# Attention into two feed-forward stages: the opening's order of work, first key loads and zero fills

## The chip, the core and the metric

The kernel runs on one core of a Trainium2 chip. The metric is the device time of one execution in microseconds (us), as the median of the runs shown. The engines are TensorE (PE, matrix products and transposes through it), VectorE (DVE), ScalarE (ACT), GpSimd (POOL) and SyncE (SP, which issues most transfers). Each works through its own instructions in order, and they wait for one another by semaphores.

## The reference

Two batches, eight heads, 768 tokens, head size 64. Queries meet the keys of a window and, beside them, one key per block of 32 (the blocks' maxima); values likewise (the blocks' means). The result, 1536 tokens by 512, goes through two dense stages.

```python
def _attn_ref(q, k, v):
    k_sum = k.reshape(B, H, nb, block, D).max(axis=3)
    v_sum = v.reshape(B, H, nb, block, D).mean(axis=3)
    scores_l = scale * np.matmul(q, k.transpose(0, 1, 3, 2))
    mask_l = np.abs(pos[:, None] - pos[None, :]) < window
    scores_s = scale * np.einsum('bhsd,bhnd->bhsn', q, k_sum)
    scores_s = scores_s + np.log(block)
    scores_l_m = np.where(mask_l, scores_l, -1000000000.0)
    scores_all = np.concatenate([scores_l_m, scores_s], axis=-1)
    scores_all = scores_all - np.max(scores_all, axis=-1, keepdims=True)
    a = np.exp(scores_all)
    a = a / (np.sum(a, axis=-1, keepdims=True) + 1e-09)
    return np.matmul(a, np.concatenate([v, v_sum], axis=2))

x = attention as 1536 x 512
x = (x @ w_a) * (x @ w_b) @ w_out      # 512 -> 1536 -> 512
h = x @ w_in                           # 512 -> 2048
out = np.maximum(0.01 * h, h) @ w_out2
```

## The kernel before

**Products.** Every fp32 product of the dense stages is three products of split operands (`mm3`, L741): each operand is a high part and the rest. A weight is brought by SP into one of three staging buffers (`stage`, L364, tile `wst`), then split by a chain of seven steps that are queued in `bg` and taken out a few at a time: L388 on VectorE and L394 on ScalarE read the staged tile, then L400, L403 and L409 on VectorE (the last, the "join", is the last reader of the staging buffer), L416 on ScalarE makes the high part, and L419 on VectorE the rest. The weights come in the order a0, b0, a1, b1, a2, b2, a3, b3, so that the seventh, a3, takes the staging buffer of the fourth, b1.

**Attention.** The work goes by pairs i of 256-token groups. For the first chunk of 512 tokens, pair i is the pair of heads 2i and 2i+1 of batch 0, for two groups j = 0, 1. `load_k` and `load_q` bring keys and queries, `k_prep` transposes keys on TensorE (six transposes, L612, in two PSUM banks), copies them to `kts` on ScalarE (L618, L620), takes the blocks' maxima on VectorE (L623) and copies these beside the keys on GpSimd (L630). `q_prep` transposes queries (L649, L653). `scores` multiplies (L670), takes mask and row minimum on VectorE (L684, one per window) and the exponential on ScalarE (L690). `normal` divides (L699 to L701), `p_transpose` turns the weights (L711, L715), and `pv` multiplies by the windows of values in `vw` (L725) and splits the result into the high part (ScalarE, L735) and the rest (VectorE, L736) of x. The blocks' sums of values are made from `vb` (L553, L567, L589, L596) and put into `vw` by GpSimd (L224). `early(kt)` multiplies the kt-th x of chunk 0 by a0, b0, a1 and b1 (PSUM banks ps_a, ps_b and two ps_c).

**Order.** `attention_ops` gives every operation a number, PER (8) per pair plus an offset (pv is at PV, 13), and the operations are written out in the order of these numbers. A scheduler then sets each engine's order. `tc.issue_after(x)` holds the instructions under it behind x. Transposes and scores take turns on four PSUM banks, in the order in which they are written, so a later one waits for the readers of the fourth before it. The value tiles `vw`, whose unused rows must be zero, are filled by GpSimd before it makes identity and masks (L275).

Of the kernel before, what the change touches and what calls it, by code (L numbers as in the profile page):

```python
# [21 lines left out]
def kernel(  # L22
# [14 lines left out]
    P = 128  # L37
# [100 lines left out]
    def load_k(b, hp):  # L138
        if b > 0 and hp >= NP - 2:
            t = vb_whole[2 * (hp - NP) + 5].rearrange("p j d -> p (j d)")[:, 0 : NTB * 2 * D]  # L140
            t = t.rearrange("p (n c d) -> p n c d", n=NTB, c=2)
        else:
            t = q_p.tile([P, NTB, 2, D], F32, tag="k", name="k", bufs=2)
        for c in range(2):
            with behind_values(b > 0):
                nc.sync.dma_start(
                    out=t[:, :, c, :], in_=k[b, 2 * hp + c].rearrange("(n p) d -> p n d", p=P)
                )
        k_t[b, hp] = t
# [86 lines left out]
    def attention_ops():  # L236
# [3 lines left out]
        for i, p in enumerate(sum(pairs, [])):  # L240
# [5 lines left out]
            for m, (b, hp) in enumerate(dict.fromkeys(x[:2] for x in p)):  # L246
                vi, r = divmod(2 * hp, HV)
                if (b, hp) not in seen:
                    seen.add((b, hp))
                    add(-22 if b > 0 and hp >= NP - 2 else -18, LOAD, load_k, b, hp)  # L250
                    for j in range(2):
                        add(2 * m + j / 4 - 10.5 if (b, hp) == (0, NP - 1) else 2 * m + j - 12, PRODUCT, k_prep, b, hp, j)
# [21 lines left out]
    for t in vw_t:  # L274
        nc.gpsimd.memset(t, 0.0)  # L275
# [94 lines left out]
    def convert():  # L370
# [15 lines left out]
        def low():  # L386
# [6 lines left out]
            with tc.issue_after(pace["turned"].ins):  # L393
                nc.scalar.activation(  # L394
                    out=t["c"].bitcast(F32), in_=hi_w.bitcast(F32), func=AF.Abs, scale=2.0**-112
                )
# [207 lines left out]
    def k_prep(b, hp, j):  # L604
# [5 lines left out]
        with tc.issue_after(st["out"].ins) if (b, hp) == (0, NP - 1) else nullcontext():  # L610
# [12 lines left out]
        nc.vector.tensor_reduce(  # L623
            out=ks_t[hp][:, g * GT // BLK : (g + n) * GT // BLK],
            in_=ps[:, : n * GT].rearrange("p (n j) -> p n j", j=BLK),
            op=ALU.max,
            axis=AX.X,
        )
# [67 lines left out]
    def normal(i, j):  # L696
        pm, sm = st["pm", i, j]
        with behind(i == 0):
            nc.vector.tensor_scalar_add(sm, sm, 1.0e-9)  # L699
# [18 lines left out]
    def pv(i, p):  # L718
# [12 lines left out]
        for j, b, hp, g, n in runs(p):  # L731
# [3 lines left out]
            nc.scalar.copy(out=x[:, 0], in_=src)  # L735
            nc.vector.tensor_tensor(  # L736
                out=x[:, 1], in0=src, in1=x[:, 0].bitcast(F32), op=ALU.subtract
            )

# [54 lines left out]
    ops.append((2.5, LOAD, lambda: [stage() for _ in range(3)], 0))  # L794
    firsts = ((("a", 0), "a"), (("b", 0), "b"), (("a", 1), "c0"), (("b", 1), "c1"))
    for i, x in enumerate(firsts):
        ops.append((PV, LOAD, lambda x=x: first_weights(*x), 0))
    ops.sort(key=lambda o: o[:2])
    rest = []
    for o in ops:  # L800
        if o[0] <= end or o[3] < n_first:
            o[2]()
            if o[1] == PRODUCT and o[0] >= PER+0.5 and (bg or cnt["conv"] < N_FIRST):
# [495 lines left out]
```

## Time and profile before

| what | us |
|---|---|
| runs shown: lowest, median, highest | 636.07, 637.85, 638.39 |
| the profiled execution's own time | 635.28 |
| span of its trace | 633.4 |
| TensorE busy in the span | 611.6 (97%) |
| VectorE busy | 485.4 (77%) |
| ScalarE busy | 317.9 (50%) |
| GpSimd busy | 55.7 (9%) |

The page is of one execution. Its span runs from the first to the last instruction; 1.9 us of its own time lie around it. Busy shares are means over the whole span, and the stretches differ: a view by stretch says which engine is full where. A row of a timeline has the start, the length, the engine, the line, the operation with output and input, and in brackets how long the engine had been idle and for what it is thought to have waited. Where a row has several instructions, its length is from the first's start to the last's end.

### The profile page before, as it was taken

What the parts mean: (1) busy time and instruction counts of PE and PEld (TensorE: products, weight loads), DVE (VectorE), ACT (ScalarE), POOL (GpSimd) and SP (SyncE); (2) the same over time, 40 slices, a digit from 0 to 9 for tenths busy, and PEclk for the clock granted to TensorE, in tenths of its full rate; (3) what the DMA queues carried; (4) which work ended last, traced back from release to release, by engine and by line L of the source; (5) the groups of instructions that cost most, each with busy time, mean ns of one, the idle gap of its engine ahead of it and who ended that gap; (6) DMA issues with size and microseconds to landing.
All of it is one profiled execution on the core that took longest, in us unless ns stands there. A gap on an engine that the chain in (4) does not pass through costs nothing.

```text
span 633.4 us, 9456 instructions
## 1 busy us (share of the span) xinstructions
PE 611.6 (97%) x3344; PEld 498.5 (79%) x3344; DVE 485.4 (77%) x1070; ACT 317.9 (50%) x707; POOL 55.7 (9%) x101
## 2 busy tenths in 40 slices
PE   6589999999999999999999999999999999999997
PEld 4467777777888888888888888877888888888886
DVE  4996987853996869986889999687588576885552
ACT  5677885752545425434453648475463434443320
POOL 5224010000000001202120102000000000000000
PEclk9899999999999999999999999999999999999999
DMA  8989757620124503736593327323133013030013
GB/s 200 257 208 199 160 116 177 191 72 24 45 71 145 136 15 94 139 120 146 142 222 102 89 80 166 95 64 109 35 99 100 14 54 99 1 99 1 0 68 132
DMA packets 81006, 67.85 MB, mean 107 GB/s; under 512 B 47360, under 2 KB 67840, under 8 KB 80960
## 3 DMA queue, kind: packets, MB, share of 16 engines
q1 hardware_dynamic: 75808, 57.95, 31.7%
q0 software_dynamic: 5152, 9.31, 8.8%
q8 instruction: 26, 0.43, 0.3%
q14 instruction: 20, 0.16, 0.1%
HBM read 52.82 MB, written 10.49 MB: 100 GB/s over the span
## 4 chain that ended last, share of the span: by engine, by line
PE 80%; DVE 5%; DMA 5%; ACT 4%; issue 3%; SPq 1%; POOL 1%; POOLq 0%; DVEq 0%; ACTq 0%
PE ps_t L743 34%; PE ps_c L743 17%; PE ps_a L743 12%; PE ps_b L743 11%; PE ps_t L670 2%; DMA wst<-in_moe_w_out_dram 2%; PE ps_t L725 1%; PE ps_t L711 1%; ACT pm L690 1%; DMA neg<-wc 1%; DMA wst<-in_moe_w_a_dram 1%; DVE wc L403 1%; DMA q<-in_q_dram 1%; DVE wc L409 1%; SPq L209 1%
## 5 line engine op out<-in xcount | busy, mean ns | idle before, releaser
L743 PE MATMUL ps_c<-wsp,hs 128*128 128x512 f32 x288 | 75.1, 390 | 1.4 <-ACT acc L860 1.0
L743 PE MATMUL ps_t<-wsp,hs 128*128 128x512 f32 x288 | 74.5, 389 | 0.0
L743 PE MATMUL ps_t<-ys,wsp 128*128 128x512 f32 x270 | 68.2, 389 | 0.0
L394 ACT ACTIVATE wc<-wst 128x512 f32<-128x512 f32 x68 | 45.3, 673 | 45.2 <-DVE wsp L419 17.8
L743 PEld LDWEIGHTS ps_c<-wsp,hs 128*128 128x128 f32 x288 | 53.9, 188 | 13.3 <-ACT acc L860 1.4
L871 DVE TENSOR_TENSOR hs<-h,hs 128x512 fp32r<-128x512 f32 x72 | 49.3, 687 | 18.6 <-ACT hs L870 18.3
L743 PEld LDWEIGHTS ps_t<-wsp,hs 128*128 128x128 f32 x288 | 54.1, 188 | 11.2
L743 PEld LDWEIGHTS ps_t<-ys,wsp 128*128 128x128 f32 x270 | 50.7, 188 | 10.5
L870 ACT CAST hs<-h 128x512 fp32r<-128x512 f32 x72 | 44.5, 621 | 26.0 <-DVE h L1134 18.4
L416 ACT CAST wsp<-wc 128x512 fp32r<-128x512 f32 x68 | 41.8, 620 | 30.6 <-DVE wc L409 30.6
L743 PE MATMUL ps_a<-x,wsp 128*128 128x512 f32 x186 | 51.2, 403 | 4.5 <-ACT x L735 4.1
L743 PE MATMUL ps_t<-x,wsp 128*128 128x512 f32 x222 | 53.2, 389 | 0.0
L743 PE MATMUL ps_b<-x,wsp 128*128 128x512 f32 x192 | 51.7, 398 | 0.0
L1086 DVE TENSOR_TENSOR h<-ps_t,h 128x512 f32<-128x512 f32 x56 | 37.6, 687 | 17.0 <-PE ps_t L743 16.7
L1022 ACT ACTIVATE h<-h 128x512 f32<-128x512 f32 x32 | 20.2, 632 | 57.5 <-DVE h L1086 57.4
L743 PEld LDWEIGHTS ps_t<-x,wsp 128*128 128x128 f32 x222 | 41.7, 188 | 8.6
L403 DVE SCALAR_TENSOR_TENSOR wc<-wc,wr 128x512 int32<-128x512 int32 x68 | 46.5, 686 | 0.7
L409 DVE SCALAR_TENSOR_TENSOR wc<-wst,wc 128x512 int32<-128x512 int32 x68 | 46.6, 686 | 0.6
L743 PEld LDWEIGHTS ps_a<-x,wsp 128*128 128x128 f32 x186 | 33.9, 188 | 13.4 <-ACT x L735 4.6
L419 DVE TENSOR_TENSOR wsp<-wc,wsp 128x512 fp32r<-128x512 f32 x56 | 38.7, 697 | 5.8 <-ACT wsp L416 5.8
L743 PE MATMUL ps_t<-hs,wsp 128*128 128x512 f32 x144 | 42.7, 389 | 0.0
L690 ACT ACTIVATE pm<-pm,nb 128x128 f32<-128x128 f32 x96 | 37.5, 393 | 10.1 <-DVE nb L684 10.0
(129 smaller groups left out, 1098.1 us busy)
## 6 DMA issues: line engine op xcount, KB each, us to landing
wst<-in_moe_w_out_dram SPq DMA_DIRECT2D x28, 512.0 KB, 3.4
wst<-in_moe_w_in_dram SPq DMA_DIRECT2D x16, 512.0 KB, 3.8
wst<-in_moe_w_a_dram SPq DMA_DIRECT2D x12, 512.0 KB, 4.8
wst<-in_moe_w_b_dram SPq DMA_DIRECT2D x12, 512.0 KB, 4.0
y<-acc POOLq DMA_DIRECT2D x16, 256.0 KB, 6.1
y<-acc SPq DMA_DIRECT2D x12, 256.0 KB, 2.3
neg<-wc POOLq DMA_DIRECT2D x12, 256.0 KB, 3.5
acc<-y SPq DMA_DIRECT2D x12, 256.0 KB, 3.1
```

The source lines that it names most:

```text
L394: nc.scalar.activation(out=t["c"].bitcast(F32), in_=hi_w.bitcast(F32), func=AF.Abs, scale=2.0**-112)
L403: nc.vector.scalar_tensor_tensor(out=t["c"], in0=t["c"], scalar=3, in1=t["r"], op0=ALU.logical_shift_left, op1=ALU.bitwise_or,)
L409: nc.vector.scalar_tensor_tensor(out=t["c"], in0=hi_w, scalar=SIGN, in1=t["c"], op0=ALU.bitwise_and, op1=ALU.bitwise_or,)
L416: t["high"] = nc.scalar.copy(out=t["w"][:, 0], in_=t["c"].bitcast(F32))
L419: nc.vector.tensor_tensor(out=t["w"][:, 1], in0=t["c"].bitcast(F32), in1=t["w"][:, 0].bitcast(F32), op=ALU.subtract,)
L670: nc.tensor.matmul(out=ps[h, w, :], lhsT=qt[h, w * W : (w + 1) * W], rhs=kts[h, (g * G + w) * SC : (g * G + w) * SC + P], start=True, stop ...
L690: nc.scalar.activation(out=pm[:, w, :], in_=pm[:, w, :], func=AF.Exp, scale=-1.0, bias=nb[:, w : w + 1], accum_out=sm[:, w : w + 1],)
L743: nc.tensor.matmul(out=ps, lhsT=w(a), rhs=x(b), start=first and j == 0, stop=last and j == 2)
L870: pace["split"] = nc.scalar.copy(out=t[:, 0], in_=src)
L871: nc.vector.tensor_tensor(out=t[:, 1], in0=src, in1=t[:, 0].bitcast(F32), op=ALU.subtract)
L1022: nc.scalar.activation(out=h, in_=src, func=AF.Prelu, alpha=0.01)
L1086: nc.vector.tensor_tensor(out=out, in0=ps, in1=u, op=ALU.add)
```

## The change

Four things are changed, in the order of the diff below.

- **First keys.** The keys of heads 0 and 1 come in four transfers and not two: blocks 0 to 3 and blocks 4 and 5 apart, head 0 issued by SP as before, head 1 by ScalarE ahead of its table load.
- **Third pair's keys.** The load of heads 4 and 5 stands behind the first two staged weights and not ahead of them. Their transposes, and those of heads 6 and 7, are held behind the first pair's pv, and the maxima of heads 4 and 5 behind the rest of the first x (L736).
- **Zeros.** VectorE fills `vw`, ahead of its other fills.
- **First x.** Only a0's conversion is begun ahead of the first pv. ScalarE's first step (L394) of every later weight is held behind the high part of the first x (L735), the second group's normalization of pair 1 behind its rest (L736), and a1 is staged by a step of its own.

The numbers of instructions stay: two fills go from GpSimd to VectorE, and two transfers more are issued.

```diff
@@ load_k
-            with behind_values(b > 0):
-                nc.sync.dma_start(
-                    out=t[:, :, c, :], in_=k[b, 2 * hp + c].rearrange("(n p) d -> p n d", p=P)
-                )
+            src = k[b, 2 * hp + c].rearrange("(n p) d -> p n d", p=P)
+            parts = ((0, 2 * GT // P), (2 * GT // P, NTB)) if (b, hp) == (0, 0) else ((0, NTB),)
+            put = nc.scalar if (b, hp, c) == (0, 0, 1) else nc.sync
+            for n0, n1 in parts:
+                with behind_values(b > 0):
+                    put.dma_start(out=t[:, n0:n1, c, :], in_=src[:, n0:n1])
@@ attention_ops
-                    add(-22 if b > 0 and hp >= NP - 2 else -18, LOAD, load_k, b, hp)
+                    add(-22 if b > 0 and hp >= NP - 2 else -13.4 if (b, hp) == (0, 2) else -18, LOAD, load_k, b, hp)
-                        add(2 * m + j / 4 - 10.5 if (b, hp) == (0, NP - 1) else 2 * m + j - 12, PRODUCT, k_prep, b, hp, j)
+                        at = {(0, 2): j / 4 - 2.5, (0, 3): j / 4 - 10}.get((b, hp), 2 * m + j - 12)
+                        add(at, PRODUCT, k_prep, b, hp, j)
@@
-        nc.gpsimd.memset(t, 0.0)
+        nc.vector.memset(t, 0.0)
@@ low, in convert
-            with tc.issue_after(pace["turned"].ins):
+            with tc.issue_after(pace["turned"].ins if i < 1 else pace["first x"].ins):
@@ k_prep
-        with tc.issue_after(st["out"].ins) if (b, hp) == (0, NP - 1) else nullcontext():
+        with tc.issue_after(st["out"].ins) if b == 0 and hp >= 2 else nullcontext():
...
+        with tc.issue_after(st["low x"].ins) if (b, hp) == (0, 2) else nullcontext():
             nc.vector.tensor_reduce(
@@ normal
-        with behind(i == 0):
+        after = st["low x"].ins if (i, j) == (1, 1) else line[-1]
+        with tc.issue_after(after) if i == 0 or (i, j) == (1, 1) else nullcontext():
@@ pv
+            if i == 0:
+                pace["first x"], st["low x"] = hi, lo
@@
-    ops.append((2.5, LOAD, lambda: [stage() for _ in range(3)], 0))
+    ops.append((2.5, LOAD, lambda: [stage() for _ in range(2)], 0))
+    ops.append((2.7, LOAD, stage, 0))
...
-        ops.append((PV, LOAD, lambda x=x: first_weights(*x), 0))
+        ops.append((PV if i < 1 else PV + 0.5, LOAD, lambda x=x: first_weights(*x), 0))
...
-            if o[1] == PRODUCT and o[0] >= PER+0.5 and (bg or cnt["conv"] < N_FIRST):
+            n_now = 1 if o[0] < PV else N_FIRST
+            if o[1] == PRODUCT and o[0] >= PER+0.5 and (bg or cnt["conv"] < n_now):
```

The scheduler makes new orders of these. TensorE's start of the program, before (line numbers of the kernel before; the four PSUM banks are ps_t, with a number for each use, and kts_91 holds heads 0 and 1):

```order
L612 MATMUL ps_t_187<-ident,k 128x128 x4
L612 MATMUL ps_t_195<-ident,k 128x128 x2
L649 MATMUL ps_t_208<-ident,q 128x128 x4
L612 MATMUL ps_t_217<-ident,k 128x128 x4
L612 MATMUL ps_t_225<-ident,k 128x128 x2
L670 MATMUL ps_t_235<-kts_91,qt 64x128 x8
L649 MATMUL ps_t_264<-ident,q 128x128 x4
L670 MATMUL ps_t_277<-kts_91,qt 64x128 x8
L612 MATMUL ps_t_297<-ident,k 128x128 x4
```

and with the change (line numbers are three to six higher there):

```order
L615 MATMUL ps_t_189<-ident,k 128x128 x4
L615 MATMUL ps_t_197<-ident,k 128x128 x2
L653 MATMUL ps_t_210<-ident,q 128x128 x4
L674 MATMUL ps_t_234<-kts_91,qt 64x128 x8
L615 MATMUL ps_t_219<-ident,k 128x128 x4
L615 MATMUL ps_t_227<-ident,k 128x128 x2
L653 MATMUL ps_t_263<-ident,q 128x128 x4
L674 MATMUL ps_t_279<-kts_91,qt 64x128 x8
L674 MATMUL ps_t_349<-kts_92,qt 64x128 x8
```

The six transposes of the second keys (ps_t 217 and 225 before, 219 and 227 now) stood ahead of the first scores and stand behind them; the third keys' transposes have left this place.

VectorE around the join of the fourth weight, b1, before (L409 is the join; in the lists of VectorE the minima of the scores of pair 2 are left out):

```order
L699 TENSOR_SCALAR sm<-sm 128x4
...
L553 TENSOR_TENSOR vb_103<-vb_103 96x512
L409 SCALAR_TENSOR_TENSOR wc<-wst,wc 128x512
L700 RECIPROCAL sm<-sm 128x4
L400 TENSOR_SCALAR wc<-wc 128x512
L567 TENSOR_REDUCE v_567<-vb_103 96x32 x2
L736 TENSOR_TENSOR x_1_654<-ps_t_637,x_1_654 128x512
```

and with the change, where the join is L412:

```order
L556 TENSOR_TENSOR vb_103<-vb_103 96x512
L704 TENSOR_SCALAR sm<-sm 128x4
L406 SCALAR_TENSOR_TENSOR wc<-wc,wr 128x512
L403 TENSOR_SCALAR wc<-wc 128x512
L570 TENSOR_REDUCE v_569<-vb_103 96x32 x2
L705 RECIPROCAL sm<-sm 128x4
...
L412 SCALAR_TENSOR_TENSOR wc<-wst,wc 128x512
L406 SCALAR_TENSOR_TENSOR wc<-wc,wr 128x512
```

The join now has the sums of values (L570), one reciprocal (L705) and the fifth weight's L403 ahead of it, which stood behind it.

ScalarE from the second value sums on to the third x (x_2), before; the second L394 here is the seventh weight's, a3:

```order
L596 ACTIVATE vs<-ps_t_661 24x256
L653 ACTIVATE qt<-ps_t_710 128x512
L394 ACTIVATE wc<-wst 128x512
L416 CAST wsp<-wc 128x512
L715 COPY pt<-ps_t_671 128x512
L690 ACTIVATE pm,sm<-pm,nb 128x128 x3
L715 COPY pt<-ps_t_732 128x512
L690 ACTIVATE pm,sm<-pm,nb 128x128
L394 ACTIVATE wc<-wst 128x512
L690 ACTIVATE pm,sm<-pm,nb 128x128 x4
L735 CAST x_2_776<-ps_t_759 128x512
```

and with the change, where L397 is that step, the first of the two the sixth weight's:

```order
L419 CAST wsp<-wc 128x512
L397 ACTIVATE wc<-wst 128x512
L720 COPY pt<-ps_t_673 128x512
L397 ACTIVATE wc<-wst 128x512
L657 ACTIVATE qt<-ps_t_712 128x512
L694 ACTIVATE pm,sm<-pm,nb 128x128 x4
L720 COPY pt<-ps_t_734 128x512
L694 ACTIVATE pm,sm<-pm,nb 128x128 x4
L720 COPY pt<-ps_t_790 128x512
L740 CAST x_2_778<-ps_t_761 128x512
```

The seventh weight's first step stood behind the first group's exponentials (L690) of pair 3, and now stands ahead of them and of the fifth queries' copy.

## Rows read from the trace of the kernel before

**Rows 1.** Busy time by stretch of the span; columns are on its first line.

```profile
core 0: us, PE busy (x) PEld busy (x) DVE busy (x) ACT busy (x) POOL busy (x), PEclk, DMA share, GB/s
15.00:30.00 15.00, 8.30 (x90) 6.05 (x88) 14.93 (x45) 10.64 (x34) 3.04 (x3) 0.92 0.90 243
45.00:60.00 15.00, 14.02 (x159) 10.97 (x159) 10.58 (x49) 11.96 (x48) 8.14 (x10) 1.00 0.94 218
120.00:400.00 280.00, 280.00 (x1355) 230.35 (x1354) 226.26 (x434) 136.76 (x261) 24.98 (x28) 1.00 0.42 110
```

**Rows 2.** Timeline of VectorE to 34 us: start, length, instruction, in brackets idle before.

```profile
8.79 1.02 DVE L623 TENSOR_REDUCE ks<-ps_t 128x16 f32<-128x512 f32 x2 [1.45 <-ACT kts L620]
10.56 0.29 DVE L684 CUSTOM_DVE_ANT_0 pm<-ps_t,negm_first 128x128 f32<-128x128 f32 x1 [0.75 <-PE ps_t L670]
...
12.08 0.29 DVE L684 CUSTOM_DVE_ANT_0 pm<-ps_t,negm_mid 128x128 f32<-128x128 f32 x1 [0.58 <-PE ps_t L670]
...
33.03 0.43 DVE L388 TENSOR_SCALAR wr<-wst 128x512 int32<-128x512 uint32 x1 [1.07 <-DMA wst<-in_moe_w_b_dram]
33.80 0.43 DVE L400 TENSOR_SCALAR wc<-wc 128x512 f32<-128x512 f32 x1 [0.34 <-ACT wc L394]
```

**Rows 3.** Timeline of TensorE, first keys and scores.

```profile
4.51 1.51 PE L612 MATMUL ps_t<-ident,k 128*128 128x128 f32 x6 [4.51 <-POOL negm_mid L288]
...
8.43 1.97 PE L670 MATMUL ps_t<-kts,qt 64*64 64x128 f32 x16
...
10.94 1.09 PE L670 MATMUL ps_t<-kts,qt 64*64 64x128 f32 x16
```

**Rows 4.** Timeline of SyncE's queue, the first key transfers.

```profile
0.74 1.02 SPq L146 DMA_DIRECT2D k<-in_k_dram  x2
```

**Rows 5.** Transfers into k issued before 2 us, issue to landing.

```profile
DMA to landing us min/median/max: 2.4/2.8/3.1
```

**Rows 6.** Timeline of GpSimd, the zeros and the first copied key sums.

```profile
0.74 1.84 POOL L275 MEMSET vw<- 128x1024 f32 x2 [0.29 <-POOLq L1281]
...
7.62 0.42 POOL L630 COPY kts<-ks 128x288 f32<-128x288 f32 x1
```

**Rows 7.** Timeline of ScalarE, copies of the second keys and first exponentials.

```profile
8.11 0.48 ACT L618 COPY kts<-ps_t 128x384 f32<-128x384 f32 x1 [0.60 <-PE ps_t L612]
8.49 0.27 ACT L620 COPY kts<-ps_t 128x128 f32<-128x128 f32 x1
...
10.89 0.40 ACT L690 ACTIVATE pm<-pm,nb 128x128 f32<-128x128 f32 x1 [1.80 <-DVE nb L684]
...
12.06 0.57 ACT L653 ACTIVATE qt<-ps_t 128x512 f32<-128x512 f32 x1
```

**Rows 8.** Timeline of VectorE, what stands behind the fourth weight's join.

```profile
39.18 0.68 DVE L409 SCALAR_TENSOR_TENSOR wc<-wst,wc 128x512 int32<-128x512 int32 x1
...
39.87 0.39 DVE L400 TENSOR_SCALAR wc<-wc 128x512 f32<-128x512 f32 x1
40.19 1.10 DVE L567 TENSOR_REDUCE v<-vb 96x32 f32<-96x256 f32 x2
```

**Rows 9.** Transfers into wst issued from 14 to 60 us, issue to landing.

```profile
DMA to landing us min/median/max: 4.9/5.9/6.8
```

**Rows 10.** Timeline of ScalarE, seventh weight, exponentials and third x.

```profile
48.00 0.68 ACT L394 ACTIVATE wc<-wst 128x512 f32<-128x512 f32 x1 [0.38 <-DVE nb L684]
48.58 0.39 ACT L690 ACTIVATE pm<-pm,nb 128x128 f32<-128x128 f32 x1
...
50.12 0.56 ACT L735 CAST x<-ps_t 128x512 fp32r<-128x512 f32 x1
50.63 0.60 ACT L653 ACTIVATE qt<-ps_t 128x512 f32<-128x512 f32 x1
```

**Rows 11.** Timeline of TensorE, the first product of the first x.

```profile
27.67 0.80 PE L743 MATMUL ps_a<-x,wsp 128*128 128x512 f32 x1 [3.64 <-ACT x L735]
```

**Rows 12.** Busy time and granted clock from 27.6 to 30.8 us.

```profile
27.60:30.80 3.20, 3.13 (x17) 2.52 (x19) 3.20 (x7) 1.99 (x7) 0.00 (x0) 0.50 1.12 279
```

More of the change, by code (lines that the diff above doesn't have):

```diff
@@ L622, in k_prep @@
         )
[L623 to L628, printed above, removed]
+        with tc.issue_after(st["low x"].ins) if (b, hp) == (0, 2) else nullcontext():
+            nc.vector.tensor_reduce(
+                out=ks_t[hp][:, g * GT // BLK : (g + n) * GT // BLK],
+                in_=ps[:, : n * GT].rearrange("p (n j) -> p n j", j=BLK),
+                op=ALU.max,
+                axis=AX.X,
+            )
         if g + n == NGB:
@@ L734, in pv @@
             x = x_tile(c, hp)[:, :, t0 : t0 + n * GT]
-            nc.scalar.copy(out=x[:, 0], in_=src)
-            nc.vector.tensor_tensor(
+            hi = nc.scalar.copy(out=x[:, 0], in_=src)
+            lo = nc.vector.tensor_tensor(
                 out=x[:, 1], in0=src, in1=x[:, 0].bitcast(F32), op=ALU.subtract
             )
+            if i == 0:
+                pace["first x"], st["low x"] = hi, lo
     def mm3(ps, w, x, first, last):
```

## The prediction

> **What bounds the kernel now.** I read the busy time by stretch first. From 120 to 400 us TensorE is busy for all 280 us, and from 45 to 60 for 14.02 of 15; from 15 to 30 it is busy for 8.30 only, while VectorE is for 14.93 of 15 [rows 1]. So the end is set by TensorE's work, and time can be won or lost only ahead of some 50 us. There VectorE sets the pace: its timeline shows no gap from 12.08, the minima of the second scores, until it waits 1.07 and 0.34 for the fourth weight at 33 us [rows 2]. What this dense run loses or gains goes through x into TensorE's products, and from there one for one to the end. All four edits lie in this part.
>
> **Start.** The first keys land 2.4 and 3.1 after their issues; SP issues both in 1.02, so at 0.74 and about 1.25, and they land at 3.1 and 4.35 [rows 4, 5]. TensorE's first transposes begin at 4.51, put down to GpSimd, but the second landing is as late [rows 3]. With two queues both issues can stand at 0.74. The gain lies between nothing (the engines that carry the bytes are as full as before) and 4.35 - 3.1 = 1.25; I take 0.8, since the other head's blocks 0 to 3 are all that the first four transposes need. The trace shows with this pair what sharing does: the second landing took 0.7 longer than the first from its issue. The Trainium skill (DMA: Bandwidth & Descriptors, Issuing engines are not separate DMA queues) says that transfers from several engines run on the same 16 DMA engines and that a second issuer saves only the time of issuing; by it the gain would be one issue's half of 1.02, 0.5, and the sum 0.3 higher.
>
> GpSimd would hold this gain up: its first copy of key sums starts at 7.62, right behind its masks, and these began behind 1.84 of zeros [rows 6]. Without the zeros they end by 5.8, and the keys decide. The zeros on VectorE have no row. Between the first instruction at 0.7 and the first maxima, which cannot come before TensorE's transposes at 3.7, VectorE has 3 us for them; as on GpSimd they would take 1.84, and if they were half that, nothing changes. Cost nothing, while they stay below 2. So the first scores come at 7.6 for 8.43 [rows 3], the first minima at 9.75 for 10.56, and the first exponential at 10.1 for 10.89 [rows 2, 7].
>
> **Second keys.** Here the change loses it. Their transposes used TensorE's time ahead of the first scores, and their maxima stood at 8.79 [rows 2]. Now they stand behind these scores, which take 1.97 [rows 3], and ScalarE has three exponentials ahead of their copies: 10.89 to 12.06 before, 1.17 [rows 7]. So the first copies start at 10.1 + 1.17 = 11.25, take 0.65 (8.11 to 8.76) [rows 7], and the first of the two maxima (half of 1.02 and some) ends at 12.5. The second scores wait for that, as they use its PSUM bank. From their start at 10.94 to their minima at 12.08 it was 1.14 [rows 2, 3], so now 13.6. **The dense run begins 1.5 later.** It could be none, if copies or transposes came sooner, and 2.3 if the keys don't land earlier.
>
> **Third pair's keys and first x.** Transposes, copies and maxima are the same in number, later, and inside the dense run: no cost on VectorE. VectorE has fewer steps ahead of the first x's rest, so x comes earlier; TensorE waited 3.64 for it [rows 11]. But b0's rest comes later, and TensorE's next products need that, so I count nothing for the early x by itself. What is won is the wait for the fourth weight: SP issues it with one value load fewer ahead of it, and VectorE meets it later; 1.07 + 0.34 = **1.4 won** [rows 2].
>
> **The seventh weight.** Its staging buffer comes free with the join of the fourth, b1, which ended at 39.18 + 0.60, 27.7 behind 12.08 [rows 2, 8]. The join now has another L400 (0.39) and the value sums (1.10) ahead, which were behind it [rows 8]: less the overlap, 1.4. So it ends at 13.6 + 27.7 - 1.4 + 1.4 = 41.3. Transfers into wst take 4.9 to 6.8, median 5.9 [rows 9]; the weight lands at 46.2 to 48.1, I take 47.2. Before, ScalarE began its L394 at 48.00, behind the first group's exponentials [rows 10]. Now it waits for it ahead of them, and everything behind it on ScalarE waits too: L394 0.58, the queries' copy 0.5, four exponentials 1.54 (48.58 to 50.12), a copy 0.5, four exponentials 1.54, a copy 0.5, then the third x [rows 10]. 47.2 + 5.2 = 52.4, for 50.12: **2.3 later.** VectorE, ready for these exponentials from about 46 on, idles about 2 us, having done more of the conversions.
>
> **Sum.** From the third x on TensorE has 1 us spare in 15 [rows 1], so at most 1 of this is taken up; I take none. The 1.5 and the 1.4 are in the 2.3 already. 635.28 + 2.3 = 637.6 on the profiled execution. The median of the runs shown stands 2.57 above that one: 637.85 + 2.3 = **640.2**.
>
> **Rivals.** *A: faster, no wait at the seventh weight.* If the second keys' copies slip in so that the dense run begins at 12.1 as before, the join ends at 39.8, the transfer can land by 44.7 (4.9), ahead of the exponentials, and what stays is 1.4 won and 1.4 of work brought forward: -2.8, or 635.0; should TensorE also fill a part of its 3.64, 634.3. It decides at the second minima: 12.1 or 13.6. For it speaks that the keys may gain 1.25; against it, that three exponentials stand in the way in the written order. *B: no change.* VectorE's work is the same, and 1.5 lost against 1.4 won is nothing; the weight lands at 46.2 and TensorE's 1 us of spare takes what is left: 637.9. *C: slower by twice as much.* The first scores took 1.97, the later ones 1.09, for the same work [rows 3], and after the wait of 3.64 the granted clock stood at 0.50 (1.2 GHz) from 27.6 to 30.8 [rows 11, 12]. TensorE's opening now has the second keys' transposes (1.51) standing later and two gaps. If the low clock lasts over the second scores too, these and the transposes cost 0.9 + 0.7 more; with keys that gain nothing (0.8) and a seventh weight at the late end (0.8) the sum is 2.3 + 3.2 = 5.5: 643.4. The Trainium skill (TensorE: Matmul & The Clock Gate, Part 1) says that the array starts at half rate and gets the full rate only after sustained work; that this trace shows at its start by the 1.97. *D: the change doesn't do what it says:* the keys land no earlier, all else as forecast: 641.0, inside the range.
>
> **Chances.** Forecast 0.47 (639 to 642), A 0.18, B 0.15, C 0.20. A measurement of this kernel can tell 0.5%, 3.2 us, from no change: below 634.7 is faster, above 641.0 slower. Faster: most of A, 0.14. Slower: C, and the upper third of the forecast with D, 0.37. The same: 0.49. The range, 634.8 to 643.8, holds A's upper part, B, the forecast, and C up to its price.
>
> **What would show it.** Right: first transposes at about 3.7, the second minima at 13.6, b1's join at 41.3, ScalarE idle ahead of L397 until 47.2, the third x's high part at 52.4, and VectorE idle there. Wrong: second minima by 12.1, or a seventh L397 that waits for no transfer, or the products after 60 us standing where they did although the third x is late; then TensorE had room that I did not see. The start's part is wrong if the first transposes still begin at 4.5, the zeros' if VectorE's first maxima wait for its fills.

## The result: 1.2% slower, and the profile after

| what | before | with the change |
|---|---|---|
| median of the runs, us | 637.03 (636.07 to 638.39) | 644.82 (643.84 to 645.21) |
| ratio, 95% interval | | 1.0118 (1.0093 to 1.0144) |
| profiled execution, us | 635.28 | 643.84 |
| span of its trace, us | 633.4 | 642.1 |
| TensorE / VectorE / ScalarE busy, us | 611.6 / 485.4 / 317.9 | 619.3 / 486.6 / 317.8 |

The forecast of 640.2 was 2.3 above 637.85, the median that stands ahead of it. The direction was the forecast's, the size was not: 7.8 us lost where 2.3 were forecast, and 644.82 is one above the range. First, where the time is lost: busy time by stretch, with the change.

```profile
core 0: us, PE busy (x) PEld busy (x) DVE busy (x) ACT busy (x) POOL busy (x), PEclk, DMA share, GB/s
15.00:30.00 15.00, 9.71 (x84) 7.30 (x83) 14.40 (x43) 10.23 (x37) 2.43 (x2) 0.77 0.94 247
30.00:45.00 15.00, 13.76 (x89) 9.43 (x90) 10.95 (x34) 6.10 (x18) 3.34 (x4) 0.54 0.69 177
45.00:60.00 15.00, 12.80 (x137) 9.82 (x135) 10.20 (x43) 11.30 (x40) 5.71 (x7) 1.00 1.04 221
```

From 30 to 45 us VectorE idles for four of 15 us and ScalarE for nine. TensorE is busy for 13.76, but with 89 products only, at a granted clock of 0.54, that is for the most part at the lower level, 1.2 GHz; before, the same stretch held 123, at 0.97:

```profile
30.00:45.00 15.00, 12.87 (x123) 9.62 (x120) 13.56 (x41) 9.16 (x27) 1.80 (x3) 0.97 0.85 206
```

TensorE's timeline with the change (start, length, instruction, idle before) has the marks of the opening. L749 is L743 of before.

```profile
3.71 1.51 PE L615 MATMUL ps_t<-ident,k 128*128 128x128 f32 x6 [3.71 <-DMA k<-in_k_dram]
...
7.45 1.97 PE L674 MATMUL ps_t<-kts,qt 64*64 64x128 f32 x16 [0.78 <-ACT qt L657]
...
26.57 0.49 PE L749 MATMUL ps_a<-x,wsp 128*128 128x512 f32 x1 [0.87 <-ACT x L740]
...
31.79 1.97 PE L674 MATMUL ps_t<-kts,qt 64*64 64x128 f32 x16 [1.16 <-POOL kts L634]
...
47.69 0.48 PE L749 MATMUL ps_a<-x,wsp 128*128 128x512 f32 x1
...
72.22 3.03 PE L749 MATMUL ps_a<-x,wsp 128*128 128x512 f32 x12
```

The last two of these stood in the timeline of before at 39.82 and 64.00. So the first x is earlier by 1.1 (26.57 for 27.67 [rows 11]), the second later by 7.9, and the run after the fourth x later by 8.2. Behind that mark the spans hold 569.9 and 569.4: of the 8.7 by which the spans differ all but 0.5 is lost ahead of it, nearly all ahead of the second x, and TensorE gives nothing back. VectorE's timeline shows what it waited for; L412 is the join, L570 the sums of values, and the row at 44.26 has the first of the minima that stand ahead of the second x.

```profile
1.02 0.91 DVE L278 MEMSET vw<- 128x1024 f32 x1 [1.02 <-PEq L1289]
2.10 0.91 DVE L278 MEMSET vw<- 128x1024 f32 x1 [0.16 <-issue]
...
13.61 0.29 DVE L688 CUSTOM_DVE_ANT_0 pm<-ps_t,negm_mid 128x128 f32<-128x128 f32 x1 [0.75 <-PE ps_t L674]
...
34.51 0.43 DVE L391 TENSOR_SCALAR wr<-wst 128x512 int32<-128x512 uint32 x1 [2.45 <-DMA wst<-in_moe_w_b_dram]
...
41.21 0.43 DVE L391 TENSOR_SCALAR wr<-wst 128x512 int32<-128x512 uint32 x1 [1.60 <-DMA wst<-in_moe_w_a_dram]
...
43.16 1.09 DVE L570 TENSOR_REDUCE v<-vb 96x32 f32<-96x256 f32 x2
...
44.26 0.26 DVE L688 CUSTOM_DVE_ANT_0 pm<-ps_t,negm_mid 128x128 f32<-128x128 f32 x1
...
45.08 0.68 DVE L412 SCALAR_TENSOR_TENSOR wc<-wst,wc 128x512 int32<-128x512 int32 x1
...
54.52 0.17 DVE L704 TENSOR_SCALAR sm<-sm 128x4 f32<-128x4 f32 x1 [3.58 <-ACT pm L694]
```

VectorE waits for two weights, not one: the fourth, b1, at 34.51 (before 1.07 and 0.34 [rows 2]) and the fifth, a2, at 41.21, which before came in time. ScalarE waits for the fifth and for the seventh, a3, each time ahead of work that was ready (L397 is L394 of before):

```profile
41.27 0.68 ACT L397 ACTIVATE wc<-wst 128x512 f32<-128x512 f32 x1 [1.86 <-DMA wst<-in_moe_w_a_dram]
41.85 0.57 ACT L720 COPY pt<-ps_t 128x512 f32<-128x512 f32 x1
...
46.62 0.57 ACT L740 CAST x<-ps_t 128x512 fp32r<-128x512 f32 x1
...
51.80 0.67 ACT L397 ACTIVATE wc<-wst 128x512 f32<-128x512 f32 x1 [2.39 <-DMA wst<-in_moe_w_a_dram]
...
57.90 0.58 ACT L740 CAST x<-ps_t 128x512 fp32r<-128x512 f32 x1
```

These rows add up to the lateness of the second x. Before, the same minima and its high part stood here (VectorE, then ScalarE), and VectorE's busy time from the second minima to them was, before and with the change:

```profile
37.66 0.28 DVE L684 CUSTOM_DVE_ANT_0 pm<-ps_t,negm_mid 128x128 f32<-128x128 f32 x1
...
38.73 0.56 ACT L735 CAST x<-ps_t 128x512 fp32r<-128x512 f32 x1
```

```profile
12.08:37.66 25.58, 16.55 (x180) 12.50 (x180) 23.99 (x73) 17.34 (x59) 3.79 (x4) 0.93 0.92 235
13.61:44.26 30.65, 23.83 (x181) 16.90 (x177) 25.93 (x80) 16.94 (x56) 5.17 (x6) 0.68 0.84 215
```

The second minima are 1.5 later. From there VectorE idles 3.1 longer (4.72 for 1.59) and works 1.9 longer (25.93 for 23.99) until the minima that the second x stands behind, and from these to the x ScalarE takes 1.3 longer (2.36 for 1.07), as four exponentials now stand ahead of it there where one did. Together that is 7.9. From the second x to the run after the fourth, 25.60 pass with the change and 25.27 before: the later waits, the one for a3 too, add next to nothing.

SP's queue shows why the weights are late. With the change (b1, then a2, then a3):

```profile
26.52 0.44 SPq L367 DMA_DIRECT2D wst<-in_moe_w_b_dram  x1
27.06 4.99 SPq L211 DMA_DIRECT2D vw<-in_v_dram  x6
32.09 3.81 SPq L158 DMA_DIRECT2D q<-in_q_dram  x4
35.95 0.46 SPq L178 DMA_DIRECT2D vb<-in_v_dram  x1
36.52 0.37 SPq L367 DMA_DIRECT2D wst<-in_moe_w_a_dram  x1
...
45.82 0.39 SPq L367 DMA_DIRECT2D wst<-in_moe_w_a_dram  x1
```

and before (b1, two loads of values, a2):

```profile
26.95 0.37 SPq L364 DMA_DIRECT2D wst<-in_moe_w_b_dram  x1
27.41 1.15 SPq L209 DMA_DIRECT2D vw<-in_v_dram  x2
28.67 1.33 SPq L364 DMA_DIRECT2D wst<-in_moe_w_a_dram  x1
```

Between b1 and a2 stood two loads; now eleven do, and a2's issue comes 7.9 later. Its buffer was free 5 us earlier: the join of b0, the second L412, began at 30.77 and takes 0.68. And b1, issued no later than before, took longer to land:

```profile
DMA to landing us min/median/max: 8.0/8.0/8.0
```

That is beyond every transfer of [rows 9], whose longest took 6.8; before, b1 took 6.1.

### The profile page after: what moved, and what is told of

Read it like the earlier page. It is cut to its first block, busy times and chain, and to the rows that moved or that the text cites. A ratio compares the mean times of both kernels' runs of the same rounds, so it can differ in the third digit from the quotient of the medians.

```text
span 642.1 us, 9458 instructions
## 1 busy us (share of the span) xinstructions
PE 619.3 (96%) x3344; PEld 503.2 (78%) x3344; DVE 486.6 (76%) x1072; ACT 317.8 (49%) x707; POOL 53.6 (8%) x99
## 4 chain that ended last, share of the span: by engine, by line
PE 77%; DVE 5%; issue 3%; DMA 2%; ACT 1%; ACTq 0%; POOLq 0%; DVEq 0%
PE ps_t L749 32%; PE ps_c L749 18%; PE ps_a L749 11%; PE ps_b L749 11%; DMA neg<-wc 2%; PE ps_t L674 2%; PE ps_t L730 1%; PE ps_t L716 1%; DVE h L1094 1%; ACT pm L694 1%; DVE wc L406 1%; DVE acc L871 0%; DVE hs L879 0%; DVE wc L412 0%; DVE h L1142 0%
## 5 line engine op out<-in xcount | busy, mean ns | idle before, releaser
L749 PE MATMUL ps_c<-wsp,hs 128*128 128x512 f32 x288 | 75.1, 390 | 0.5 <-ACT wsp L438 0.4
L749 PE MATMUL ps_t<-wsp,hs 128*128 128x512 f32 x288 | 74.5, 389 | 0.0
L749 PE MATMUL ps_t<-ys,wsp 128*128 128x512 f32 x270 | 68.2, 389 | 0.0
L397 ACT ACTIVATE wc<-wst 128x512 f32<-128x512 f32 x68 | 45.1, 672 | 43.2 <-DVE wsp L422 15.4
L749 PEld LDWEIGHTS ps_c<-wsp,hs 128*128 128x128 f32 x288 | 53.9, 188 | 12.5 <-ACT wsp L438 0.8
L749 PEld LDWEIGHTS ps_t<-wsp,hs 128*128 128x128 f32 x288 | 54.1, 188 | 11.3
L749 PEld LDWEIGHTS ps_t<-ys,wsp 128*128 128x128 f32 x270 | 50.7, 188 | 10.5
L749 PE MATMUL ps_t<-x,wsp 128*128 128x512 f32 x222 | 53.2, 389 | 0.0
L749 PE MATMUL ps_a<-x,wsp 128*128 128x512 f32 x186 | 50.5, 400 | 1.8 <-ACT x L740 1.7
L749 PE MATMUL ps_b<-x,wsp 128*128 128x512 f32 x192 | 51.8, 400 | 0.0
L749 PEld LDWEIGHTS ps_t<-x,wsp 128*128 128x128 f32 x222 | 41.7, 188 | 8.7
L412 DVE SCALAR_TENSOR_TENSOR wc<-wst,wc 128x512 int32<-128x512 int32 x68 | 46.6, 687 | 0.6
L391 DVE TENSOR_SCALAR wr<-wst 128x512 int32<-128x512 uint32 x68 | 28.6, 423 | 18.9 <-ACT wsp L438 8.9
L749 PE MATMUL ps_t<-hs,wsp 128*128 128x512 f32 x144 | 42.7, 389 | 0.0
```

The source lines that it names most:

```text
L391: nc.vector.tensor_scalar(out=t["r"], in0=lo_w.bitcast(U32), scalar1=2.0**-29, scalar2=7.0, op0=ALU.mult, op1=ALU.min,)
L397: nc.scalar.activation(out=t["c"].bitcast(F32), in_=hi_w.bitcast(F32), func=AF.Abs, scale=2.0**-112)
L412: nc.vector.scalar_tensor_tensor(out=t["c"], in0=hi_w, scalar=SIGN, in1=t["c"], op0=ALU.bitwise_and, op1=ALU.bitwise_or,)
L749: nc.tensor.matmul(out=ps, lhsT=w(a), rhs=x(b), start=first and j == 0, stop=last and j == 2)
```

## The experiments

Each ratio is to the kernel before, run beside it on the same chip. In the short diffs, - is the kernel that is named, and `...` stands for lines or words left out.

**Each part undone or alone.** From the change, the part on the first x is taken out (place_undone: `pace["turned"]`, three weights staged at 2.5, `behind(i == 0)`, conversions begun ahead of the first pv); to the kernel before that part alone is added (place_alone), the first keys with the zeros (keys_alone), the third pair's keys (third_alone), the zeros (zeros_alone).

```diff
place_undone, from the change
-            with tc.issue_after(pace["turned"].ins if i < 1 else pace["first x"].ins):
+            with tc.issue_after(pace["turned"].ins):
...
zeros_alone, from before
-        nc.gpsimd.memset(t, 0.0)
+        nc.vector.memset(t, 0.0)
```

> The changed kernel without its fourth part: all four first weights are converted ahead of the first pv as before, and nothing is held behind the first x but the third keys' maxima. Staging theory: the fourth part delays the join of b0 by some 9 us, so that a2's transfer is issued at 36.5 and not at 28.7, and ScalarE, standing before a2's first step, holds the copy that the second x needs; without this part a2 is issued near 29, the second x comes at 39 to 40, and the time is within 2 us of before. Second-keys theory: the dense run of VectorE still begins at 13.6 and not at 12.1, and the time stays 3 us or more above before. Clock theory: the granted clock between 15 and 45 us stays near 0.6, and so does the loss, 5 us or more.

> The kernel before with the fourth part only. Staging theory: b0's join is late here too, a2's transfer is issued at 34 to 37, the second x comes 5 to 8 us late, and the time is 4 to 8 us above before, although the second scores' minima stand at 12.1. Second-keys theory: within 2 us of before. Clock theory: slower only if the granted clock between 15 and 45 us falls under 0.7.

> The kernel before with the four pieces of the first keys and the zeros on VectorE only. The second keys' transposes stand behind the first scores here as in the changed kernel. Staging theory: the second minima at about 13.6, and at most 1.5 us lost at the end. Second-keys theory: the 1.5 us grow on their way, 3 us or more at the end. The first transposes should begin at 3.7 in both.

> The kernel before with the third pair's keys later only. Staging theory: b0's join stands where it did within 2 us, and the time is within 2 us of before. Second-keys theory: the same. Clock theory: TensorE has a longer idle between 14 and 20 us without these transposes; if the granted clock falls for it, 3 us or more above before.

> The kernel before with the zeros on VectorE only; every other engine keeps its order, GpSimd's masks start 1.84 us earlier. The fills take 1.8 us in VectorE's wait before the first maxima: no cost. The first scores waited for GpSimd, so they may come up to 0.3 us earlier; the time is the same within 1 us. If the kernel before loses to any shift of its start, as the other three parts did by themselves (0.8 to 1.3%), 3 us or more are lost here too.

| kernel | median, us | ratio (95%) | profiled run, us | second minima | high part of x 1, 2, 3, 4 | run after the fourth x |
|---|---|---|---|---|---|---|
| before | | | 635.28 | 12.08 | 27.05, 38.73, 50.12, 58.58 | 64.00 |
| the change | 644.82 | 1.0118 (1.0093 to 1.0144) | 643.84 | 13.61 | 25.96, 46.62, 57.90, 66.69 | 72.22 |
| place_undone | 644.27 | 1.0164 (1.0123 to 1.0205) | 641.72 | 13.35 | 26.78, 43.27, 57.94, 65.06 | 70.56 |
| place_alone | 642.56 | 1.0132 (1.0097 to 1.0168) | 642.11 | 13.20 | 26.09, 37.99, 55.01, 64.20 | 69.70 |
| keys_alone | 641.64 | 1.0106 (1.0056 to 1.0156) | 643.48 | 14.29 | 28.71, 41.05, 55.13, 65.42 | 70.83 |
| third_alone | 639.89 | 1.0081 (1.0056 to 1.0107) | 636.17 | 11.21 | 24.79, 39.20, 52.14, 60.58 | 65.96 |
| zeros_alone | 638.95 | 1.0025 (1.0001 to 1.0049) | 638.95 | 12.04 | 27.69, 39.63, 50.95, 59.35 | 64.76 |

The marks are of one profiled run each, and the runs of one kernel lie 1 to 6 us apart (638.70 to 644.66 in after_fifth_held_filled), so a mark is one sample: third_alone's is of a run 3.7 under its median and doesn't hold its loss. The three larger parts cost 0.8 to 1.3% each, 3.2% if added; together they cost 1.2%. The traces suggest why they don't add up: each delays x by waits of its own in the same stretch. With the first x's part alone the second x is even early, and the third is 4.9 late. With the keys alone the a3 wait that I forecast appears, although only the start was changed:

```profile
51.00 0.66 ACT L396 ACTIVATE wc<-wst 128x512 f32<-128x512 f32 x1 [3.91 <-DMA wst<-in_moe_w_a_dram]
```

The staging theory of the expectations fails: taking the part on the first x out of the change does not give the loss back; a2 is issued at 31.66 there and not near 29, and VectorE waits 1.71 for b1 and 2.14 for a2. Nor was third_alone within 2 us, and in place_alone and keys_alone the second minima came 1.1 and 0.7 later than expected. The zeros alone cost 0.25%, by an interval that hardly clears nothing, with the orders of TensorE, ScalarE and SP as they were; the run after the fourth x is only 0.8 late there.

**The fifth weight's first step behind the copy that the second pv needs.** If ScalarE's place for a2 makes the second x late, this gives it back.

```diff
after_fifth_held, from the change
-            with tc.issue_after(... else pace["first x"].ins):
+            with tc.issue_after(... else st["pt copy"].ins if i == 4 else pace["first x"].ins):
-            n_now = 1 if o[0] < PV else N_FIRST
+            n_now = 1 if o[0] < PV else N_FIRST - 1 if o[0] < PER + PV else N_FIRST
```

> The changed kernel, but the fifth weight's conversion (a2) begins only behind the second pair's pv is written, and its first step on ScalarE is held behind the copy that this pv needs; the seventh weight's first step then stands behind the first group's exponentials of pair 3 too. In-order theory: the loss is ScalarE and VectorE standing in order before a weight that has not landed (1.86 and 1.60 us for a2, 2.39 and 3.58 for a3 in the changed kernel), with work behind it that was ready; the second x comes at 41 to 43 and not at 46.6, and the time falls by 3 to 6 us against the changed kernel, to within 5 us of before. Transfer theory: the opening is bound by what the DMA engines can carry; the weights land no earlier, the third x stays near 57, and the time stays within 1.5 us of the changed kernel.

Measured: 641.15, ratio 1.0086 (1.0047 to 1.0126). The run after the fourth x is 3.0 earlier, at 69.22; second x 43.23, third 52.76 (the forecast had 52.4), b1's join ended at 41.1 (forecast 41.3). The a2 wait on VectorE is gone and b1's is 1.07. Then the next thing is late, the load of queries, and with it the fourth x (63.71, 11 behind the third; before 8.5, with the change 8.8). TensorE's timeline there:

```profile
55.23 0.41 PE L653 MATMUL ps_t<-ident,q 128*128 128x128 f32 x2 [1.21 <-DMA q<-in_q_dram]
```

So this place was worth 3.0 us in the marks of one run each; the median stands 0.3% of the time nearer to before, and its interval overlaps the change's.

**The fifth weight issued early, or buffers of their own.** If the transfers' issue is the cause, an early issue gives most of it back.

```diff
after_fifth_early, from the change
+        if key == ("a", 2):
+            t = g_p.tile([P, 2, T], I32, tag="gs", name="wst", bufs=M1).rearrange("p a t -> p (a t)")
...
+        held = tc.issue_after(late["b1"].ins) if key == ("a", 2) else nullcontext()
...
after_own4, from the change
+        if key in (("a", 2), ("b", 2), ("a", 3), ("b", 3)):
+            t = g_p.tile([P, 2, T], I32, tag="gs", name="wst", bufs=M1).rearrange("p a t -> p (a t)")
...
before_fifth_late, from before
+        if key == ("a", 2):
+            late["b2"] = wst_p.tile([P, 1024], I32, tag="wst", name="wst")
+        if key == ("b", 2):
+            t = late.pop("b2")
```

> The changed kernel with buffers of their own for the fifth to eighth weights (a2, b2, a3, b3), in space that is free then: their transfers no longer wait for the joins of earlier weights. Staging theory: a2 is issued before 30 and lands before 38, ScalarE does not wait for a2 or a3, and the time falls by 4 us or more against the changed kernel. Transfer theory: the weights share the DMA engines with the loads of values and queries and push these back; x comes later instead, and the time falls by 1 us at most or rises. In-order theory: between them, as the order on ScalarE stays.

> The changed kernel with a buffer of its own for the fifth weight (a2) and its transfer issued right behind the fourth's, not twelve transfers later; the order on ScalarE stays, a2's first step ahead of the copy for the second pv. Weights theory: a2 is issued at 27 and lands by 36, ScalarE and VectorE no longer wait for it (1.86 and 1.60 us), the second x comes at 42 to 44 and not at 46.8, and the time falls by 2 us or more, as it did with the step moved on ScalarE. If the wait only moves to another transfer (the loads of values or the sixth weight), the time stays within 1 us of the changed kernel's 1.2% above before.

> The kernel before with the order of every engine as it is, but the fifth and sixth weights' staging buffers exchanged: a2 goes where a1 was, and must wait for a1's join (31.3) and not b0's (26.4), so its transfer is issued at 32 and not at 28.7, and the loads behind it in SyncE's queue are later too. Weights theory: a2 lands at 38 to 39, ScalarE waits for it ahead of the second x or VectorE does, and 2 us or more are lost. If the place of the transfers has 3 us of slack, the time is the same within 1 us.

after_fifth_early: 644.74, ratio 1.011 (1.0073 to 1.0147). There a2 is issued at 27.20, right behind b1, and VectorE still waits for it:

```profile
36.57 0.43 DVE L398 TENSOR_SCALAR wr<-wst 128x512 int32<-128x512 uint32 x1 [1.54 <-DMA wst<-in_moe_w_a_dram]
```

9.3 from issue to landing: 9.3 us early bought 4.6 us. The second x is 1.2 earlier, the end is not. after_own4: 644.13, ratio 1.0108 (1.0067 to 1.0148); there the scheduler put b1 behind a2, b2 and a3, at 30.03, and VectorE and ScalarE waited 2.85 and 3.12 for it at 39.3. before_fifth_late (the kernel before, a2 and b2 meant to exchange buffers): 636.51, ratio 0.9986 (0.996 to 1.0012); a2 was still issued at 29.18 there and not at 32 as meant, so it is no test. An earlier issue alone is not the cure.

**Less to transfer.** Two kernels leave out most of the value loads (`vw`) of pairs 1 to 3 of batch 0's first groups, so their second to fourth x are not the reference's.

```diff
+        if b == 0 and 0 < hp and g == 0:
+            rows(WIN, W, 0, 1)
+            return
```

> The changed kernel without most of the loads of values into vw for the pairs 1 to 3 of the first batch (each pair's first rows alone are loaded): 1.1 MB less of some 13 MB in the first 60 us, a sixth of their packets. Transfer theory: this gives back 4 us or more, and brings the changed kernel within 3 us of the kernel before with the same loads left out. In-order theory: the waits for a2 and a3 get shorter, but 5 us or more stay between the two.

> The kernel before with the same loads left out. Transfer theory: it gains less than the changed kernel, 0 to 2 us, since little of its opening waits for transfers (1.07 and 3.16 us for the fourth weight). In-order theory: as much as the changed kernel within 2 us, so that the distance of the two stays.

With the change 643.6, ratio 1.0109 (1.006 to 1.0157); before 636.56, ratio 1.0002 (0.9979 to 1.0025). The distance stays, so these loads, by the expectation a sixth of the packets, don't make it. Yet this changed kernel's profile tells something more, though it is of one run of 646.4, 2.8 above the median: b1 is issued at 24.44 and lands in 5.9, VectorE waits neither for b1 nor for a2, and the second x is at 45.39 all the same. On TensorE, GpSimd and VectorE (three timelines of that kernel):

```profile
34.34 3.24 PE L677 MATMUL ps_t<-kts,qt 64*64 64x128 f32 x26 [3.73 <-POOL kts L637]
```

```profile
32.86 0.97 POOL L180 DMA_DIRECT2D vb<-in_v_dram  x1 [10.29 <-DVE ks L630]
33.87 0.42 POOL L637 COPY kts<-ks 128x288 f32<-128x288 f32 x1
```

```profile
36.36 0.29 DVE L691 CUSTOM_DVE_ANT_0 pm<-ps_t,negm_first 128x128 f32<-128x128 f32 x1 [2.46 <-PE ps_t L677]
```

Where the weight was on time here, the third pair's keys were not: their key sums, which GpSimd copied at 16.29 before, are now copied at 33.87, behind a load that GpSimd issues, and TensorE waits 3.73 for them. The move of these keys, which I had counted at nothing, is in this kernel a second bound right behind the weights.

**The second keys' transposes ahead of the first scores, as before.** This takes back the 1.5 of the forecast's second term.

```diff
after_second_keys_first, from the change
...
+                with tc.issue_after(st["turned", 0, 1].ins) if (i, j) == (0, 0) else nullcontext():
                     nc.tensor.matmul(out=ps[h, w, :], ...
```

> The changed kernel with the first scores held behind the second keys' transposes, as the kernel before has them; nearly all else keeps its place. Second-keys theory: the second minima come at 12 and not at 13.6, VectorE's dense run begins 1.5 us earlier, and the time falls by 1.5 us or more. Staging theory: the run ends earlier, but it then waits longer for the fourth and fifth weights, whose transfers don't come earlier: 0 to 1 us. Clock theory: 0 to 1 us, and the granted clock from 30 to 45 us stays near 0.55.

The second minima come at 12.40, 1.2 earlier, and nothing is won that the intervals tell: 643.36, ratio 1.0098 (1.0067 to 1.0128). VectorE meets the weights sooner and waits the longer (a run of 644.52):

```profile
35.31 0.43 DVE L391 TENSOR_SCALAR wr<-wst 128x512 int32<-128x512 uint32 x1 [4.22 <-DMA wst<-in_moe_w_b_dram]
...
43.39 0.43 DVE L391 TENSOR_SCALAR wr<-wst 128x512 int32<-128x512 uint32 x1 [3.53 <-DMA wst<-in_moe_w_a_dram]
```

**The clock.** Of the 8.22 that the mark at 72.22 is late, TensorE's busy time up to it takes 7.65 (55.76 for 48.11, at a mean clock of 0.86 for 0.97). That looks like rival C. Two tests: transposes of the identity that fill TensorE's gaps (14 ahead of the first pv, 20 behind the first product; after_filled1 has the 14 alone), and the change once more, unaltered.

```diff
+            for _ in range(N_IDLE[0]):
+                with tc.issue_after(turned.ins):
+                    turned = nc.tensor.transpose(idle[:, 0:P], ident, ident)
...
```

> The changed kernel with 14 transposes of the identity more, into a bank that is free, in TensorE's wait of 2.3 us for the value sums (16.3 to 18.6). Clock theory: that wait, in which the third keys' transposes stood before, is where the granted clock falls; with it filled the clock stays at 1.00 until at least 28 us, TensorE's steps from 18 to 46 us take half as long, its busy time grows by some 2 us from the transposes and falls by 5 to 7 from the clock, and the time falls by 3 us or more. In-order theory: the clock rises, but the second and third x come when they did, within 1 us, as they wait for VectorE and the weights; the time falls by 1 us at most.

> The same with 20 more such transposes behind the first x's products with a0, where TensorE waits 1.8 and 1.2 us for the third keys. Clock theory: the clock stays at 1.00 until 46 us too, and the time falls by 4 us or more against the changed kernel. In-order theory: 1 us at most, or the transposes themselves cost up to 1 us.

> The kernel before with both such fills. Its clock was at 0.92 and 0.97 of full from 15 to 45 us, so the clock theory expects little here: 0 to 2 us gained. In-order theory: the same or up to 1 us lost. If it loses 3 us or more, filling itself costs, or moves the order of other instructions, and the two runs with fills say nothing of the clock.

> The changed kernel once more, unedited, beside these two on the same chip: 1.0 to 1.4% above before, with the granted clock under 0.8 somewhere between 15 and 45 us in the profiled execution.

after_filled1: clock 0.96 from 15 to 30 and 0.70 from 30 to 45; 644.04, ratio 1.0108 (1.0082 to 1.0134); in its profiled run, of 641.96, the second x is at 44.37 and the run after the fourth at 70.57. after_filled: 0.94 and 0.84; 641.43, ratio 1.0072 (1.0045 to 1.0099), but its orders on TensorE and ScalarE moved too. before_filled: 641.76, ratio 1.0076 (1.0055 to 1.0097): the same fills cost the kernel before 5 us, so they move more than the clock, and say nothing certain of it. The repetition is the better test. Its one profile had a different clock by itself:

```profile
30.00:45.00 15.00, 9.97 (x85) 6.86 (x84) 10.31 (x30) 5.76 (x16) 2.96 (x4) 0.78 0.71 181
```

3.8 us less TensorE time in that stretch than in the first profile, and the second x is no earlier, 46.97 for 46.62; the run after the fourth x is at 72.58 for 72.22, the time 644.07, ratio 1.0122 (1.0088 to 1.0155). In the first profile TensorE was full from 32 to 44, in this one it waited there. So the slow products of this stretch lay beside the waits for the weights and don't make the second x late. The stretch behind it tells the same: from 45 to 60 the clock was 1.00 in the first profile and 0.88 in this one, and from the second x to the run after the fourth it took 25.60 and 25.61.

Over the kernels the loss doesn't go with the clock either. From 15 to 45 us its mean was 0.94 before and 0.66 with the change, but 0.83 in before_fewer_values and 0.84 in before_fifth_late, which lose nothing, 0.89 in place_alone, which loses 1.3%, and 0.94 in after_fifth_held_filled, which loses 0.7% (each of one profile). In both profiles of the change it was 0.77 from 15 to 30; after_filled1, with 0.96 there, gains nothing in the median.

**Cures together.** a2's step held and the fills (after_fifth_held_filled), and with the second keys first as well (after_all_three).

> The changed kernel with both remedies together: the fifth weight's first step behind the copy that the second pv needs, and TensorE's two waits filled with transposes (14 and 20). Both theories together (a low clock and in-order waits for weights, each of which hides the other): the clock over 0.9 from 15 to 45 us and no wait of ScalarE for a2 or a3, the second x by 41.5, the third by 52, and the time at least 2 us under that of either remedy alone, within 3 us of before. If one of them alone were the cause, this run would gain no more than that remedy alone did (3 us at most for each): 4 to 5 us above before.

> The same with the second keys' transposes ahead of the first scores too. By itself that moved the dense run 1.2 us earlier and gave nothing, as the weights were waited for instead. Both theories together: with those waits gone it gives up to 1.2 us, so that the time is within 2 us of before. Transfers still binding: nothing, the time as in the run without it, and a longer wait of VectorE for the fourth weight.

641.41, ratio 1.0067 (1.0041 to 1.0093), and 641.57, ratio 1.0088 (1.0055 to 1.0121). In the second VectorE waits only 0.91 for b1 and no more for a2 (ScalarE still 1.12), the second minima are at 11.69, the second x at 40.72, 2.0 behind the one before; and TensorE waits for GpSimd, 1.36 for copied key sums at 39.78, and at the third pv for copied value sums:

```profile
51.09 1.15 PE L737 MATMUL ps_t<-pt,vw 128*64 128x64 f32 x32 [1.86 <-POOL vw L226]
```

No kernel that keeps the parts comes down to the one before.

## Why the prediction failed

- **Start: right.** The first transposes begin at 3.71 (forecast 3.7), the first scores at 7.45 (7.6). In all thirteen kernels here with the new key loads the first transposes begin at 3.51 to 3.91, in the seven without, zeros_alone among them, at 4.19 to 4.68. The Trainium skill (DMA: Bandwidth & Descriptors, Issuing engines are not separate DMA queues) says that a second issuing engine saves only the time of issuing; by that 0.5 would have been won, an estimate from half of SP's 1.02, and 0.80 was. That the cut into pieces made the difference is argued, not shown: no run has the pieces without the second engine.
- **Zeros: right.** 0.91 each on VectorE, ended at 3.0, ahead of keys that landed later; alone 0.25%, half of the 0.5% that I had said a measurement can tell.
- **Second minima: right to the point, and no price by themselves.** 13.61 for 13.6. But in the changed kernel "the dense run begins 1.5 later" has no price that after_second_keys_first can tell: the run has waits for transfers in it, and in that trace those grew by more than was won ahead of them (4.22 and 3.53 for 2.45 and 1.60). In the kernel before, the keys' part alone did cost 1.1%.
- **"1.4 won" at the fourth weight: this step failed.** I expected a wait to vanish because SP would issue b1 one load sooner and VectorE would meet it later. SP issued it 0.4 sooner, it landed 8.0 behind its issue, beyond every row I had, and VectorE waited 2.45.
- **The fifth weight: missing from the sum.** Of a step that the change moves I should have followed every issue. The order of SP's queue was there to be read: a2 stood eleven loads behind b1 instead of two. The 1.60 on VectorE and 1.86 on ScalarE are its wait. These two steps account for the size: I had put 27.7, with no wait in it, from the second minima to the end of b1's join; it took 45.08 + 0.68 - 13.61 = 32.15, 4.45 more, and VectorE's waits in between are 2.45 + 1.60, with 0.50 for ScalarE at 21.00: 4.55.
- **The seventh weight: right in kind, 4.5 late.** ScalarE waits for it ahead of ready exponentials, VectorE idles behind that for 3.58. The join ends at 45.8 and not at 41.3; that moves its landing to 51.7 from 47.2 and the third x to 57.90 from 52.4. From landing to third x the forecast had 5.2; it took 6.1. But the second x, for which the sum had no term, was as late already: the third stands 11.3 behind it, 11.4 before.
- **"No cost" for the third pair's keys, and nothing counted for the first x's place: wrong.** 0.8% and 1.3% alone.
- **Rivals.** C had the time nearly (643.4), but its place is not where the time went: the second scores took no longer (2.02 for 32 products, where the first took 1.97 for 16), their minima were on time, and the low clock of 30 to 45 us doesn't hold the second x. That its price came within 1.4 of the measured time is luck. D fell with the keys, which came earlier. A needed the join by 39.8 and fell; so did B.

**What stays open.** Shown: nearly all of the loss lies ahead of the second x, and it passes on one for one; in this trace it is the sum of a later start, longer waits for b1 and a2, more work of VectorE and a longer order on ScalarE; no single part, transfer or clock level that was tried holds it. One pair of profiles has moving a2's step on ScalarE worth 3.0, which the medians don't confirm. Argued only: that the remaining 4 to 5 us are one bundle of bounds close behind one another (b1's and a2's landing, the third pair's key sums and the value sums on GpSimd, the queries), of which each experiment removed the first. Why b1's transfer took 8.0 isn't settled: with fewer value loads it took 5.9, without any gain at the end.

## What to carry to other kernels

In a tightly scheduled opening, follow each staged transfer through the issuing queue, not only its buffer: count what stands between its issue and the one before it, in both orders, and price every weight that is consumed in the stretch, not the one that looks tight. Time won ahead of a wait for a transfer can be lost again in that wait. And when an operation's preparation is moved from slack to just before its use, ask how many engines it crosses on the way (here TensorE, ScalarE, VectorE, GpSimd), since each has a queue that can hold it.

## What was not expected of the hardware

- An issue 9.3 us sooner (27.20 for 36.52) brought the same 512 KB only 4.6 us sooner (36.5 for 41.2): issue to landing was 9.3 and not 4.7, beside loads that SP issued in the same stretch.
- The same kernel was given a clock of 0.54 in one execution and 0.78 in another over the same 15 us, and the second x stood within 0.35 us of the same place.
- The low clock came behind short stalls. With the change TensorE had idled 2.29 by 18.57, and the low level lasted from about 17.6 to 24.4; it then idled 0.87, 1.77 and 1.16 between 25 and 32, and the low level lasted from about 31.2 to 44.9. In sum that is no more idle than before (0.90, 0.76, 0.99 and 3.64 between 15 and 28), where the low level lasted from 27.6 to 30.8 only [rows 12]. The Trainium skill (TensorE: Matmul & The Clock Gate, Part 1) ties the clock to how busy the array has recently been; that agrees with the falls. From 32 to 44 the profile has TensorE busy throughout and the clock at 0.50 all the while, and no run here shows why it stayed there.
- The first scores took 1.97 and the later ones 1.09 [rows 3], though the granted clock of both stretches stands at 1.00 in the profile (from 8.4 to 10.4 and from 10.9 to 12.0 us, before). With the change 16 of them took 1.97 again at 31.79, where the clock stood at 0.50: the slow start isn't seen in that figure.
